# Gated attention and MLP: a redesign in head quads with row strips, column strips and VectorE chords, where GpSimd makes the two shifted copies of each VectorE pair

## Chip, cores and metric

The kernel runs on one core of one Trainium2 chip. The metric is device time in microseconds (us) of one execution. Engines in the profile: PE is TensorE's matmuls, PEld its weight loads, DVE is VectorE, ACT is ScalarE, POOL is GpSimd, SP is the engine that issues most DMAs.

## What is computed

```python
B, S, D = 1, 2048, 640          # F = 1536, H = 32 heads, Dh = 20; all bf16
def _A_ref(x, wqkv, wo):
    qkv = (x @ wqkv).reshape(B, S, 3, H, Dh).transpose(2, 0, 3, 1, 4)
    q, k, v = qkv[0], qkv[1], qkv[2]
    scores = jnp.einsum("bhqd,bhkd->bhqk", q, k) * Dh ** -0.5
    p = softmax(scores, axis=-1)
    o = jnp.einsum("bhqk,bhkd->bhqd", p, v)
    return o.transpose(0, 2, 1, 3).reshape(B, S, D) @ wo
def _B_ref(x, w1, b1, w2):
    h = x @ w1 + b1
    return (h * jnp.tanh(softplus(h))) @ w2          # mish
x = A_x
g = sigmoid((x * gate_w).sum(-1, keepdims=True))
return g * _A_ref(x, A_wqkv, A_wo) + (1 - g) * _B_ref(x, B_w1, B_b1, B_w2)
```

The bulk is the attention: 32 heads x 2048 x 2048 scores, each of which needs an exponential. In tiles of 128 keys x 1024 (two heads x 512 queries, a "pair" below) these are 1024 pairs.

## The kernel before, in words

x is brought in transposed by one DMA (`xT`, feature on partitions). The queries are cut into four chunks of 512 (`qc`), the heads into 16 groups of two (`emit_group`). For a group the loop over `NS` = 16 key blocks makes one pair per step, in this order on PE: two score matmuls into PSUM (L395; the heads' 20 features lie on 20 of the 128 partitions, at partitions `base` and `base + 32`, so the two are row strips of the array), then eight accumulating matmuls (L412) with the pair's exponentials as weights (128x128 each) and 21 columns of V moving (20 features and a column of ones that gives the softmax denominator). Between them ACT takes the exponential of all 1024 columns in one instruction (L406). `aps` holds two score tiles and `e_pool` two exponential tiles. At a group's end DVE takes reciprocals of the denominators and scales (L421, L423).

All other work is cut into units that stand in a list: projections of Q, K and V (`qt_unit` L208, `kt_units` L143, `v_units` L186), the MLP's first matmul with its mish (`mlp_ht_unit` L223: an Exp on ACT, L231, and five DVE instructions, among them a reciprocal at L241), its second matmul (`mlp_b_units` L261), and the transposes and output projection of the query chunk before (L288, L304, L318). `pump_slot` is called after each pair with a credit of 340 or 460 and emits units by a cost written with each. So PE's order is the program's order: a pair, then some units, then a pair. Projections of K and V for a head quad are done once, in the first query chunk. The softmax scale is applied inside the exponential. Weights come by DMA from ACT's, SP's and GpSimd's queues.

Of the kernel before, what the change touches and what calls it, by code (L numbers as in the profile page):

```python
# [8 lines left out]
P = 128  # L10
ACT = mybir.ActivationFunctionType
ALU = mybir.AluOpType
F32 = mybir.dt.float32
BF16 = mybir.dt.bfloat16


@with_exitstack
def kernel(
# [12 lines left out]
    nc = tc.nc  # L31

    _, S, D = A_x.shape
    F = B_w1.shape[1]
    H = 32
    DH = D // H
    KT = D // P
    FT = F // P
    NS = S // P
    QC = 512  # L40
    NQC = S // QC
    NU = QC // P
    NPAIR = H // 4
    NG = H // 2
    ROWB = 32
    inv_sqrt_dh = float(DH) ** -0.5
    CB = 512
    CH = CB // 2

    x2d = A_x[0]  # L50
    out2d = out[0]

    consts = ctx.enter_context(tc.tile_pool(name="consts", bufs=1))
    wqp = consts.tile([P, KT, NPAIR, P], BF16, tag="wqp")
    ident = consts.tile([P, P], BF16, tag="ident")
    wo_sb = consts.tile([P, KT, D], BF16, tag="wo_sb")
    w1_sb = consts.tile([P, KT, F], BF16, tag="w1_sb")
    w2_sb = consts.tile([P, FT, D], BF16, tag="w2_sb")
    b1bf = consts.tile([P, FT], BF16, tag="b1bf")
    b1f = consts.tile([P, FT], F32, tag="b1f")  # L60
    g_t = consts.tile([P, NS], F32, tag="g_t")
    kT_all = consts.tile([P, NPAIR, S], BF16, tag="kT_all")
    VA = consts.tile([P, NS, H, DH + 1], BF16, tag="VA")

    aps = ctx.enter_context(tc.tile_pool(name="aps", bufs=2, space=bass.MemoryType.PSUM))
    xtc_pool = ctx.enter_context(tc.tile_pool(name="xtc", bufs=2))
    qtc_pool = ctx.enter_context(tc.tile_pool(name="qtc", bufs=3))
    e_pool = ctx.enter_context(tc.tile_pool(name="e_pool", bufs=2))
    opool = ctx.enter_context(tc.tile_pool(name="opool", bufs=1))
    otpool = ctx.enter_context(tc.tile_pool(name="otpool", bufs=1))  # L70
    actpool = ctx.enter_context(tc.tile_pool(name="actpool", bufs=1))
    mishp = ctx.enter_context(tc.tile_pool(name="mishp", bufs=2))
    bpool = ctx.enter_context(tc.tile_pool(name="bpool", bufs=2))
    smallp = ctx.enter_context(tc.tile_pool(name="smallp", bufs=2))
    dpool = ctx.enter_context(tc.tile_pool(name="dpool", bufs=1))
    outp = ctx.enter_context(tc.tile_pool(name="outp", bufs=2))

    xt_ctx = ExitStack()
    xt_ctx.__enter__()
    xtpool = xt_ctx.enter_context(tc.tile_pool(name="xtpool", bufs=1))  # L80
    xT = xtpool.tile([P, KT, S], BF16, tag="xT")

    stage_ctx = ExitStack()
    stage_ctx.__enter__()
    stpool = stage_ctx.enter_context(tc.tile_pool(name="stpool", bufs=1))
    Wq = stpool.tile([P, KT, D], BF16, tag="Wq")
    nc.scalar.dma_start(Wq, A_wqkv[:, 0:D].rearrange("(kt p) c -> p kt c", p=P))
    nc.sync.dma_start_transpose(
        out=xT[:, :, :], in_=x2d.rearrange("s (kt p) -> s kt p", p=P)
    )  # L90
    wv0 = xtpool.tile([P, KT, 4 * DH], BF16, tag="wvp", bufs=2)
    nc.scalar.dma_start(
        out=wv0[:, :, :],
        in_=A_wqkv[:, 2 * D : 2 * D + 4 * DH].rearrange("(kt p) c -> p kt c", p=P),
    )
    gw = xtpool.tile([P, KT, 1], BF16, tag="gw")
    nc.scalar.dma_start(gw, gate_w.rearrange("(kt p o) -> p kt o", p=P, o=1))
    wk0 = xtpool.tile([P, KT, P], BF16, tag="wkp", bufs=2)
    nc.gpsimd.memset(wk0, 0.0)
    for r in range(4):  # L100
        col0 = 64 * (r // 2) + ROWB * (r % 2)
        nc.scalar.dma_start(
            out=wk0[:, :, col0 : col0 + DH],
            in_=A_wqkv[:, D + r * DH : D + (r + 1) * DH].rearrange(
                "(kt p) c -> p kt c", p=P
            ),
        )
    nc.sync.dma_start(b1bf, B_b1.rearrange("(ft p) -> p ft", p=P))
    nc.gpsimd.dma_start(wo_sb, A_wo.rearrange("(kt p) c -> p kt c", p=P))
    nc.gpsimd.dma_start(w1_sb, B_w1.rearrange("(kt p) c -> p kt c", p=P))  # L110
    nc.gpsimd.dma_start(w2_sb, B_w2.rearrange("(ft p) c -> p ft c", p=P))

    nc.gpsimd.memset(wqp, 0.0)
    for h in range(H):
        p, r = divmod(h, 4)
        col0 = 64 * (r // 2) + ROWB * (r % 2)
        nc.gpsimd.tensor_copy(
            out=wqp[:, :, p, col0 : col0 + DH],
            in_=Wq[:, :, h * DH : (h + 1) * DH],
        )  # L120
    stage_ctx.__exit__(None, None, None)
    make_identity(nc, ident)
    nc.vector.tensor_copy(b1f, b1bf)
    nc.gpsimd.memset(VA, 1.0)

    def kt_units(p, wk=None):
        if wk is None:
            wk = xtpool.tile([P, KT, P], BF16, tag="wkp", bufs=2)
            nc.gpsimd.memset(wk, 0.0)
            for r in range(4):  # L130
                h = 4 * p + r
                col0 = 64 * (r // 2) + ROWB * (r % 2)
                nc.sync.dma_start(
                    out=wk[:, :, col0 : col0 + DH],
                    in_=A_wqkv[:, D + h * DH : D + (h + 1) * DH].rearrange(
                        "(kt p) c -> p kt c", p=P
                    ),
                )

        def chunk(sc):  # L140
            pk = aps.tile([P, CB], F32, tag="t")
            for kt in range(KT):
                nc.tensor.matmul(  # L143
                    pk[:, 0:QC],
                    lhsT=wk[:, kt, 0:P],
                    rhs=xT[:, kt, sc * QC : (sc + 1) * QC],
                    start=(kt == 0),
                    stop=(kt == KT - 1),
                )
            nc.vector.tensor_copy(  # L150
                out=kT_all[:, p, sc * QC : (sc + 1) * QC], in_=pk[:, 0:QC]
            )

        return [(1200, (lambda sc=sc: chunk(sc))) for sc in range(NQC)]

    def v_units(p, wv=None):
        if wv is None:
            wv = xtpool.tile([P, KT, 4 * DH], BF16, tag="wvp", bufs=2)
            nc.sync.dma_start(
                out=wv[:, :, :],  # L160
                in_=A_wqkv[:, 2 * D + 4 * p * DH : 2 * D + 4 * (p + 1) * DH].rearrange(
                    "(kt p) c -> p kt c", p=P
                ),
            )

        def unit(st):
            pv = aps.tile([P, CB], F32, tag="t")
            for kt in range(KT):
                lhsT = xT[:, kt, st * P : (st + 1) * P]
                if p == 0:  # L170
                    nc.tensor.matmul(  # L171
                        pv[:, 0 : 4 * DH],
                        lhsT=lhsT,
                        rhs=wv[:, kt, :],
                        start=(kt == 0),
                        stop=False,
                    )
                    nc.tensor.matmul(
                        pv[:, 4 * DH : 4 * DH + 1],
                        lhsT=lhsT,  # L180
                        rhs=gw[:, kt, 0:1],
                        start=False,
                        stop=(kt == KT - 1),
                    )
                else:
                    nc.tensor.matmul(  # L186
                        pv[:, 0 : 4 * DH],
                        lhsT=lhsT,
                        rhs=wv[:, kt, :],
                        start=(kt == 0),  # L190
                        stop=(kt == KT - 1),
                    )
            nc.vector.tensor_copy(  # L193
                out=VA[:, st, 4 * p : 4 * p + 4, 0:DH],
                in_=pv[:, 0 : 4 * DH].rearrange("p (h d) -> p h d", d=DH),
            )
            if p == 0:
                nc.scalar.activation(
                    g_t[:, st : st + 1], pv[:, 4 * DH : 4 * DH + 1], ACT.Sigmoid
                )  # L200

        return [(260, (lambda st=st: unit(st))) for st in range(NS)]

    def qt_unit(p, xTc, qTc_p):
        def unit():
            pq = aps.tile([P, CB], F32, tag="t")
            for kt in range(KT):
                nc.tensor.matmul(  # L208
                    pq[:, 0:QC],
                    lhsT=wqp[:, kt, p, 0:P],  # L210
                    rhs=xTc[:, kt, 0:QC],
                    start=(kt == 0),
                    stop=(kt == KT - 1),
                )
# [312 lines left out]
```

## Time and profile before

| | |
|---|---|
| runs | 1384.87, 1419.17, 1405.74 us; median 1405.74 |
| the profiled execution | span 1383.0 us from its first to its last instruction; its time around the span is not listed, and the nearest run, 1384.87, is 1.9 over it |
| exponentials (L406, ACT) | 1024 x 1022 ns |
| score matmuls (L395, PE) | 2048 in 1024 strips of two, 589.2 us busy |
| accumulating matmuls (L412, PE) | 8192 x 182 ns, 398.1 us busy |
| reciprocal of the MLP (L241, DVE) | 96 x 1744 ns |
| DMA | 16.91 MB, at 185 GB/s in the first fortieth of the span, 1 to 21 GB/s after the second |

The page gives for every engine its busy time and its share of the span, and cuts the span into 40 slices in which each digit is a tenth. PEclk is the clock granted to TensorE, in tenths of full. Groups of instructions give line, engine, operation, output and inputs with shapes, count, busy time and mean duration, and behind the bar the idle time before them with what ended it. Matmuls overlap in the array, so durations of single matmuls add up to more than the time they take; start-to-start distances are read from the timeline.

### The profile page before, as it was taken

How to read it: one execution, taken by the hardware profiler on the slowest of the kernel's cores; microseconds unless marked ns; L12 is line 12 of the kernel's file. 1: busy time of each engine (PE TensorE's matmuls, PEld its weight loads, DVE VectorE, ACT ScalarE, POOL GpSimd, SP SyncE). 2: the span in 40 equal slices, each digit the busy share in tenths (PEclk: the TensorE clock that was granted, in tenths of full speed). 3: DMA queues.
4: the chain of work that ended last, by engine and by line, in shares of the span. 5: the costliest groups of instructions: out<-in, count | busy, mean ns of one | idle time of the engine just before them, and what ended most of it. 6: DMA issues, size and time to landing. Idle time of an engine off the chain costs nothing.

```text
span 1383.0 us, 28359 instructions
## 1 busy us (share of the span) xinstructions
PE 1235.3 (89%) x12384; PEld 589.6 (43%) x12384; DVE 463.9 (34%) x1093; ACT 1053.3 (76%) x1138; POOL 28.6 (2%) x51
## 2 busy tenths in 40 slices
PE   0699999988999988998889998998889988998887
PEld 0354444544444444443434444443434444453333
DVE  0222222377722576410101477410001476510002
ACT  0286666987768877698998777698998787699995
POOL 7000000000000000000000000000000000000000
PEclk9975555975585555795555555695555555695555
DMA  9600000000000000000000000000000000000000
GB/s 185 109 8 7 8 7 7 2 1 1 13 8 11 11 1 1 1 21 1 1 1 11 11 1 1 1 2 1 1 2 6 16 2 1 1 2 1 1 1 20
DMA packets 53086, 16.91 MB, mean 12 GB/s; under 512 B 49408, under 2 KB 52096, under 8 KB 52960
## 3 DMA queue, kind: packets, MB, share of 16 engines
q1 hardware_dynamic: 47456, 9.30, 4.6%
q0 software_dynamic: 912, 4.75, 1.2%
q10 hardware_dynamic: 4592, 1.03, 0.6%
q8 instruction: 97, 1.59, 0.5%
q14 instruction: 29, 0.24, 0.1%
HBM read 7.21 MB, written 2.62 MB: 7 GB/s over the span
## 4 chain that ended last, share of the span: by engine, by line
PE 67%; ACT 25%; issue 3%; DMA 3%; DVE 1%; ACTq 0%
PE Sp L395 26%; ACT E L406 25%; PE acc L412 15%; PE ph L223 8%; PE pk L143 5%; PE pb L261 4%; DMA xT<-in_A_x_dram 3%; PE pq L208 3%; PE pa L304 3%; PE pv L186 3%; PE pt L288 1%; ACTq L406 0%; PE pv L171 0%; ACT e_sb L231 0%; DVE d L311 0%
## 5 line engine op out<-in xcount | busy, mean ns | idle before, releaser
L406 ACT ACTIVATE E<-Sp 128x1024 bf16<-128x1024 f32 x1024 | 1006.0, 1022 | 223.6 <-PE Sp L395 213.0
L395 PE MATMUL Sp<-qTc_p,kT_all 20*128 20x512 bf16 x2048 | 589.2, 559 | 0.0
L412 PEld LDWEIGHTS <-E 128*128 128x128 bf16 x8192 | 335.7, 106 | 471.1 <-ACT E L406 376.9
L412 PE MATMUL acc<-VA,E 128*128 128x21 bf16 x8192 | 398.1, 182 | 95.5 <-ACT E L406 93.5
L241 DVE RECIPROCAL rd<-rd 128x256 f32<-128x256 f32 x96 | 167.4, 1744 | 0.8
L395 PEld LDWEIGHTS <-kT_all 20*128 20x128 bf16 x2048 | 104.3, 98 | 51.5 <-issue 18.2
L223 PE MATMUL ph<-xTc,w_sb 128*128 128x256 bf16 x480 | 119.0, 403 | 0.1
L421 DVE RECIPROCAL rden<-acc 128x8 f32<-128x8 f32 x64 | 12.4, 193 | 297.4 <-PE acc L412 297.4
L223 PEld LDWEIGHTS <-w_sb 128*128 128x128 bf16 x480 | 51.7, 128 | 57.4 <-issue 42.6
L234 DVE SCALAR_TENSOR_TENSOR e_sb<-e_sb 128x256 f32<-128x256 f32 x96 | 40.4, 421 | 100.5 <-ACT e_sb L231 99.6
L215 DVE CAST qTc_p<-pq 128x512 bf16<-128x512 f32 x32 | 22.1, 691 | 148.8 <-PE Sp L395 98.6
L231 ACT ACTIVATE e_sb<-ph,b1f 128x256 f32<-128x256 f32 x96 | 45.4, 473 | 33.8 <-PE ph L223 29.9
L143 PE MATMUL pk<-xT,wk 128*128 128x512 bf16 x140 | 66.0, 548 | 0.0
L208 PE MATMUL pq<-xTc,wqp 128*128 128x512 bf16 x160 | 64.5, 492 | 0.0
L261 PE MATMUL pb<-w_sb,actT 128*128 128x512 bf16 x192 | 58.0, 419 | 0.1
L150 DVE CAST kT_all<-pk 128x512 bf16<-128x512 f32 x32 | 22.1, 691 | 96.3 <-PE pk L143 96.3
L186 PE MATMUL pv<-wv,xT 128*128 128x80 bf16 x560 | 50.7, 237 | 0.0
L193 DVE CAST VA<-pv 128x80 bf16<-128x80 f32 x128 | 30.4, 243 | 57.7 <-PE pv L186 51.5
L143 PE MATMUL pk<-xT,wk_118 128*128 128x512 bf16 x20 | 7.2, 544 | 44.4 <-DMA xT<-in_A_x_dram 44.4
L243 DVE SCALAR_TENSOR_TENSOR actT<-ph,b1f,rd 128x256 bf16<-128x256 f32 x96 | 45.8, 478 | 0.1
L186 PEld LDWEIGHTS <-xT 128*128 128x128 bf16 x560 | 33.4, 117 | 23.2 <-issue 23.0
L261 PEld LDWEIGHTS <-actT 128*128 128x128 bf16 x384 | 28.5, 101 | 33.3 <-issue 24.1
(101 smaller groups left out, 351.9 us busy)
## 6 DMA issues: line engine op xcount, KB each, us to landing
w_sb<-in_B_w_dram POOLq DMA_DIRECT2D x2, 1920.0 KB, 31.1
out_dram<-ot SPq DMA_DIRECT2D x16, 160.0 KB, 1.8
Wq<-in_A_wqkv_dram ACTq DMA_DIRECT2D x1, 800.0 KB, 4.9
wo_sb<-in_A_wo_dram POOLq DMA_DIRECT2D x1, 800.0 KB, 24.5
wv<-in_A_wqkv_dram SPq DMA_DIRECT2D x7, 100.0 KB, 2.3
wk<-in_A_wqkv_dram SPq DMA_DIRECT2D x28, 25.0 KB, 2.6
wv_114<-in_A_wqkv_dram ACTq DMA_DIRECT2D x1, 100.0 KB, 10.7
wk_118<-in_A_wqkv_dram ACTq DMA_DIRECT2D x4, 25.0 KB, 29.7
```

The lines of the kernel that those rows point to most:

```text
L143: nc.tensor.matmul(pk[:, 0:QC], lhsT=wk[:, kt, 0:P], rhs=xT[:, kt, sc * QC : (sc + 1) * QC], start=(kt == 0), stop=(kt == KT - 1),)
L186: nc.tensor.matmul(pv[:, 0 : 4 * DH], lhsT=lhsT, rhs=wv[:, kt, :], start=(kt == 0), stop=(kt == KT - 1),)
L208: nc.tensor.matmul(pq[:, 0:QC], lhsT=wqp[:, kt, p, 0:P], rhs=xTc[:, kt, 0:QC], start=(kt == 0), stop=(kt == KT - 1),)
L223: nc.tensor.matmul(ph[:, 0:CH], lhsT=w1_sb[:, kt, ft * P : (ft + 1) * P], rhs=xTc[:, kt, half * CH : (half + 1) * CH], start=(kt == 0), st ...
L231: nc.scalar.activation(e_sb, ph[:, 0:CH], ACT.Exp, bias=b1f[:, ft : ft + 1], scale=1.0)
L241: nc.vector.reciprocal(out=rd, in_=rd)
L243: nc.vector.scalar_tensor_tensor(out=actT[:, ft, half * CH : (half + 1) * CH], in0=ph[:, 0:CH], scalar=b1f[:, ft : ft + 1], in1=rd, op0=AL ...
L261: nc.tensor.matmul(tile_[:, 0 : col1 - col0], lhsT=actT[:, ft, u * P : (u + 1) * P], rhs=w2_sb[:, ft, col0:col1], start=(ft == 0), stop=(f ...
L304: nc.tensor.matmul(pa[:, :], lhsT=oT[:, ct, u * P : (u + 1) * P], rhs=wo_sb[:, ct, 0:CB], start=(ct == 0), stop=(ct == KT - 1),)
L395: nc.tensor.matmul(Sp[:, QC * t : QC * (t + 1)], lhsT=kT_all[base + ROWB * t : base + ROWB * t + DH, p, j * P : (j + 1) * P,], rhs=qTc_p[b ...
L406: nc.scalar.activation(E[:, :], Sp[:, :], ACT.Exp, scale=inv_sqrt_dh)
L412: nc.tensor.matmul(acc[:, u, t, 0 : DH + 1], lhsT=E[:, QC * t + P * u : QC * t + P * (u + 1)], rhs=VA[:, j, h, 0 : DH + 1], start=first, s ...
```

## The change

The kernel body is written anew. What it does:

- **Opening.** x comes in its own layout in seven plain DMAs and is transposed by PE (80 transposes) into `xT`. The weights come whole, from SP's queue.
- **Head quads.** Four heads lie on the four 32-partition strips of `kT` and `qT` (20 features, then zeros). A pass (`try_pass`, `score_mms`, L609) issues two score matmuls for one pair, or four for two pairs (heads 0 and 1 of the quad, "L", and heads 2 and 3, "R"). Key and query strips are made 128 rows at a time, written to DRAM and read back strip by strip.
- **Two kinds of exponential.** A pair in `SA` or `SB` goes to ACT (L985, as before). A pair in `SD` goes to DVE (L996): one tensor_scalar adds a bias to the scaled score, clamps at zero and converts to int16, whose bits read as bf16 are a chord of the exponential. GpSimd adds two constants to those integers (L1003, `Z[1]` and `Z[2]`), and the three tiles together stand for the exponential. Three sets of such tiles exist (`NZ`), eight tiles for ACT's (`NE`).
- **Column strips.** V with its column of ones is the weight (128 x 32), the exponentials move (512 columns), and the four heads of the quad accumulate in the four 32-partition strips of one PSUM bank (L738). An ACT pair is accumulated once, a DVE pair three times. All other matmuls but the transposes are also cut into four 32-column strips (`mm4`, L255).
- **Group end.** DVE copies the accumulator to SBUF, the denominators go to DRAM and back as 128x16, DVE takes the reciprocal, they go to DRAM and back spread over 32 partitions a head, and GpSimd multiplies (L786). The result goes to DRAM and is read back into `xT` for the output projection.
- **MLP.** Mish is an ACT function on 128x3072, four times for each half of the sequence; DVE adds the bias before it.
- **Order.** A planner at build time walks through time with a cost written for each operation (below), picks for each engine the next ready operation by priority or due time, and emits the whole program in that order. It also decides which pairs go to DVE, and chunk by chunk where the other work goes.

By the instruction order of the changed kernel: 733 pairs go to ACT and 291 to DVE; 731 score passes, of which 439 have two matmuls, 291 four and one six; 3212 accumulating matmuls; 582 shifted copies and 32 multiplications on GpSimd.

```diff
+LAT = 0.12
...
+SHIFTS = (35.0, 83.0)
+ZBIAS = 128.0 * 127 - 251.8
+ADDS_ON_POOL = True
...
+    NE, NZ = 8, 3
...
+    def mm4(outs_, lhs, rhs, start, stop):
+        for k in range(4):
+            nc.tensor.matmul(
+                outs_[k], lhsT=lhs[k], rhs=rhs[k], start=start, stop=stop,
+                tile_position=(0, 32 * k),
+            )
+    C4 = 0.225
...
+        return [
+            lambda t=t, k=k: nc.tensor.matmul(
+                S_[:, k * QC : (k + 1) * QC],
+                lhsT=kT[32 * t : 32 * t + 32, j * P : (j + 1) * P],
+                rhs=qT[32 * t : 32 * t + 32, g.c * QC : (g.c + 1) * QC],
+                start=True, stop=True, tile_position=(32 * t, 0),
+            )
+            for k, t in enumerate((t0, t0 + 1))
+        ]
...
+        op = Op("ACT", 0.946, None, [score], prio=3)
...
+        op = Op("DVE", 1.19, None, [score], prio=3)
...
+    def pe_start(now, dur, m, fn):
+        if mode[0] != m:
+            dur += 0.1
...
+                    lambda t=t, k=k, e=e, st=st, sp=end_ty: nc.tensor.matmul(
+                        acc[32 * t : 32 * t + 32, :],
+                        lhsT=VAs[(g.q // 2) % 2][:, e["j"], g.q % 2, t, :],
+                        rhs=e["ap"][:, k * QC : (k + 1) * QC],
+                        start=st, stop=sp, tile_position=(0, 32 * t),
+                    )
...
+            mu = new("POOL", 1.25, lambda: nc.gpsimd.tensor_tensor(out=o, in0=a, in1=rb, op=ALU.mult), d4, prio=0)
...
+                op.fn = lambda: nc.vector.tensor_scalar(
+                    out=Z[0], in0=SD, scalar1=ZBIAS, scalar2=0.0, op0=ALU.add, op1=ALU.max)
...
+                for k in range(2):
+                    if ADDS_ON_POOL:
+                        a = Op("POOL", 1.05, lambda k=k: nc.gpsimd.tensor_scalar(
+                            out=Z[k + 1], in0=Z[0], scalar1=SHIFTS[k], scalar2=1.0, op0=ALU.add, op1=ALU.mult), [op], prio=1)
+                    else:
+                        a = Op("DVE", 0.34, lambda k=k: nc.vector.tensor_scalar(
+                            out=Z[k + 1], in0=Z[0], scalar1=SHIFTS[k], scalar2=None, op0=ALU.add), [op], prio=2)
```

## The prediction

> **What bounds the kernel now.** I read the page's first two parts, then the costliest groups, then the timeline at two clocks, then the opening and GpSimd's few rows.
>
> ```profile
> span 1383.0 us, 28359 instructions
> ...
> PE 1235.3 (89%) x12384; PEld 589.6 (43%) x12384; DVE 463.9 (34%) x1093; ACT 1053.3 (76%) x1138; POOL 28.6 (2%) x51
> ...
> PEclk9975555975585555795555555695555555695555
> ```
>
> PE is busy 89% of the span, mostly at half clock, and ACT 76%: neither is full, since a pair goes PE, ACT, PE through two buffers and the projections and MLP stand between the pairs in PE's order. The timeline at half clock shows the alternation (start, length, what; in brackets what ended the idle time):
>
> ```profile
> 705.59 0.39 PE L412 MATMUL acc<-VA,E 128*128 128x21 bf16 x8 [0.25 <-ACT E L406]
> 705.91 0.61 PE L395 MATMUL Sp<-qTc_p,kT_all 20*128 20x512 bf16 x2
> ...
> 706.62 1.95 ACT L406 ACTIVATE E<-Sp 128x1024 bf16<-128x1024 f32 x2 [0.16 <-PE Sp L395]
> ```
>
> PE waits for ACT, then ACT for PE. Two exponentials back to back take 1.95, one 1.02 (L406's mean), so their distance is 0.93. The next timelines give PE's distances at full and at half clock:
>
> ```profile
> 601.82 0.39 PE L395 MATMUL Sp<-qTc_p,kT_all 20*128 20x512 bf16 x2
> 602.14 0.82 PE L208 MATMUL pq<-xTc,wqp 128*128 128x512 bf16 x3
> 602.80 0.35 PE L412 MATMUL acc<-VA,E 128*128 128x21 bf16 x8
> ```
> ```profile
> 748.16 0.61 PE L304 MATMUL pa<-wo_sb,oT_prev 128*128 128x512 bf16 x1
> 748.57 0.31 PE L318 MATMUL pa_9692<-wo_sb,oT_prev 128*128 128x128 bf16 x1
> ```
>
> Three 512-column matmuls start within 0.66, 0.22 each, at full clock; 0.41 at half. The two score strips run at the same time, but the next full-height matmul starts 0.32 after them: 0.10 is lost in changing over. Before a score pair about 0.08 is lost (705.59 to 705.91 is 0.32, eight starts at 0.03 are 0.24).
>
> ```profile
> 120.00:240.00 120.00, 120.00 (x1083) 54.85 (x1082) 27.41 (x94) 75.26 (x75) 1.89 (x3) 0.50 0.07 7
> 580.00:620.00 40.00, 38.98 (x489) 20.26 (x485) 5.68 (x18) 38.85 (x41) 0.00 (x0) 0.96 0.08 18
> ```
>
> These are stretches with busy time of PE, PEld, DVE, ACT, POOL, then the clock: 0.50 in the first although PE never rests, 0.96 in the second. In the first, 85 projections of 512 columns, 255 of 80, 149 score strips (20 of 128 rows, so 80 columns' worth each) and 594 x 21 columns fill 88,300 of 144,000 half-clock column times, 61%. In the second, 81 matmuls of at most 512, 82 score strips and 326 x 21 fill at most 57% of full. GpSimd's rows, with the opening:
>
> ```profile
> 4.21 4.38 POOL L113 MEMSET wqp<- 128x5120 bf16 x1
> ...
> 8.66 6.85 POOL L117 COPY wqp<-Wq 128x100 bf16<-128x100 bf16 x32
> 15.55 0.28 POOL masks.py:199 TENSOR_SCALAR_AFFINE_SELECT ident<-ident 128x128 bf16<-128x128 bf16 x1
> 15.79 9.05 POOL L124 MEMSET VA<- 128x10752 bf16 x1
> ```
> ```profile
> 0.75 43.62 DMA xT<-in_A_x_dram
> ```
>
> **The change part by part.** *ACT.* 733 exponentials x 0.93 = 682. Mish: from L406 (1024 elements, 1022 ns) and L231 (256, 473) an element costs 0.715 ns, so 3072 take 2.49, x 8 = 20. Five table loads at 1.28 (the length of the load before) are 6, twelve evictions in the opening at 0.6 are 7. Sum 715, against 1053.
>
> *PE, full clock.* Passes: 731 x (0.22 + 0.18 changeover) = 292, taking four strips to run at once as two do. Accumulations: 3212 matmuls go out in 880 calls of two to four strips, x 0.22 = 194. No column strips stand in this trace; they cost 0.22 a call if they run at once like row strips (taken, as both are strips of one array) and 0.22 a matmul if not. Projections, MLP, output: 2992 strips of 512 in fours, 748 x 0.22 = 165. 1280 strips of 160 (V): starts of 0.03, 320 x 0.12 = 36. 1152 strips of 128: 288 x 0.11 = 32. Transposes 80 x 0.1 = 8. Sum 727; with column strips one after the other 6204 x 0.22 = 1365 stands in place of 359 and the sum is 1733. At half clock (0.41): 431 + 361 + 307 + 43 + 35 + 8 = 1185.
>
> *DVE.* From 128x512 in 691 ns (L150) and 128x128 in 291 (L269) an element costs 1.04 ns, so 1024 take 1.23; 291 x 1.23 = 358. Some 150 evictions of 512 at 0.69 are 104, the smaller ones about 40. Sum 500, under the others; the MLP's 167 of reciprocal goes. It is hidden under PE, and if that cover went it would still be 200 short.
>
> *GpSimd.* 582 copies of 128x1024 int16 and 32 products. The trace has no arithmetic of this size. Memsets give 4.66 for 5632 elements, 0.83 ns each. Copies of 100 start every 0.215, the select of 128 takes 0.24 to the next start. If all beyond memset speed is fixed, a shifted copy costs 0.83 x 1.024 + 0.13 = 0.98. If all but a start of 0.03 goes by the element (1.8 ns), it costs 1.88. A line through the copy and the select (0.9 ns) gives 1.05, the value I take, since both read and write as the new operation does. A product reads two operands: between 0.56 and 1.9, taken 1.1. Sum 582 x 1.05 + 35 = 646, at the upper end 1094 + 60 = 1154. A copy's delay sits on a path too: PE's order holds the accumulation of `Z[2]` in place, and whatever stands behind it, the next score pass too, waits; ACT lives meanwhile from its two score tiles.
>
> The Trainium skill (GPSIMD Engine Reference, Performance versus the Vector engine, Engine selection) speaks against this use: elementwise arithmetic belongs on VectorE, GpSimd takes 2.6 cycles of 1.2 GHz an element with two inputs, though with one input about line rate. By its two-input figure, an estimate, a copy would take 2.22 and GpSimd's sum with the ends below would be about 1370; no row here shows such a price.
>
> *Ends.* The first exponential now starts at 64.35, behind the 43.6 transposing load. Plain loads of 160 KB land in 1.8 (`out`) and 100 KB in 2.3 (`wv`), so the first four tiles are there by about 5; four transposes with evictions (4) and two projections at half clock (5) put it near 16. At the end, after the last pass: eviction 0.7, four DMA hops at about 2 are 8, a product 1.1, five output units alternating 1.3 PE and 0.7 DVE are 10, the last store 1.8: 22, of which 4 to 6 are PE work already counted; net 18. DMA otherwise has room: 1 to 21 GB/s are used.
>
> *Sum.* Three engines come out near each other: PE 727, ACT 715, GpSimd 646, each in a fixed order with at most three to eight tiles between them. So none will run full; before, the fullest ran at 89%. 727 / 0.89 = 817, with 16 + 18 the span is 851, and with the 2 that the nearest run lies over its span 853: I say **850**. The profile before stands 1.6% under its median (1383.0 to 1405.74).
>
> **The rivals.** *A (0.57): as summed.* At 97% fill it is 784, at 80% 943.
>
> *B (0.19): GpSimd is the bound.* A copy between 1.35 and 1.88: 582 x 1.35 + 35 + 36 = 857, at 1.6 about 1010, at 1.88 1190. For it: the copy row allows it, and A leaves GpSimd only 0.3 a copy of room. Against: select and copy differ by 28 elements and only 0.025.
>
> *C (0.13): the clock stays low.* 1185 / 0.97 + 34 = 1256 at half clock throughout, (851 + 1256) / 2 = 1053 if half the time. For it: PE was busy without pause at 0.50 in the first stretch. Against: at half clock the new work fills (880 + 748) x 0.41 and 292 whole and 439 half passes, 878 of 1185 with V and the rest left out, 74%, more than the 61% that did not lift it; at full clock the same work at 0.22 is 471 of 851, 55%, in the neighbourhood of what held 0.96. The Trainium skill (TensorE: Matmul & The Clock Gate, Part 1) lets sustained PE activity open the clock. By it the sum stays at 853; the first stretch speaks against busyness alone.
>
> *D (0.09): slower, by one mechanism.* A shifted copy costs so much that GpSimd's queue alone is longer than the kernel before: 582 x p + 45 + 36 passes 1406 at p = 2.28 and 1434 at 2.33; at 2.5 it gives 1536. For it: int16 in and out with two operations was never timed here, and every Z2 holds up PE's order. Against: it needs 2.2 ns an element, beyond the 1.8 that the copies bound.
>
> *E (0.02): column strips run singly*, PE 1733 + 34, about 1770; the row strips that do run at once speak against it.
>
> **How the numbers follow.** Best single time 850. Below 770 lies about 0.04 (A nearly full), above 1220 a third of C with D and E, 0.16; so 770 to 1220. A measurement of this kernel tells 2% from no change (its runs spread by 2.4%). Faster by over 2%: A, B and C, 0.89; within 2%: 0.02 of D; slower: the rest of D and E, 0.09.
>
> **What would show it.** In the changed profile: L1003 near 1.05 mean and POOL near 75% busy (B: over 90%, and PE's accumulation waiting for POOL; D: POOL about 100% with copies over 2.3). PEclk 9 in most slices (C: 5). L985 idle a tenth of its time, ended by the score passes. The first exponential near 16. Row passes 0.40 to the next matmul, four accumulating strips starting within 0.22. I am wrong if the span is over 950 at full clock with copies near 1.05: then the fixed order itself loses more than the 11% taken.

## The result, and the profile after

The changed kernel takes 857.64 us (median of 4 runs, 856.22 to 860.18) against 1411.78 before; the ratio is 0.6211, 95% interval 0.6169 to 0.6252. The profiled execution took 857.08 with a span of 855.3.

The page's first two parts, where the lines shown of before had PE at 89%, ACT at 76% and mostly half clock:

```profile
span 855.3 us, 25648 instructions
...
PE 782.1 (91%) x10764; PEld 274.3 (32%) x10764; DVE 497.4 (58%) x586; ACT 731.3 (86%) x758; POOL 665.9 (78%) x632
...
POOL 6267999857995999976798799987729999989930
PEclk9999999999999999999999999999969999999999
```

Four engines are now above half busy, TensorE's clock is full but in one slice (620 to 641, 0.67), and GpSimd has long stretches at 9 with dips between. The groups of the two kinds of exponential and of the copies:

```profile
L1003 POOL TENSOR_SCALAR Z<-Z 128x1024 int16<-128x1024 int16 x582 | 609.1, 1047 | 140.7 <-DVE Z L996 91.8
L996 DVE TENSOR_SCALAR Z<-SD 128x1024 int16<-128x1024 f32 x291 | 355.4, 1221 | 187.0 <-PE SD L609 80.5
L985 ACT ACTIVATE E<-SA 128x1024 bf16<-128x1024 f32 x367 | 379.5, 1034 | 36.9 <-PE acc L738 18.7
...
L786 POOL TENSOR_TENSOR OT<-accS,rdB 128x512 bf16<-128x512 f32 x32 | 40.9, 1279 | 27.2 <-DMA rdB<-rD 25.4
```

A copy is 1047 ns long (1.05 was taken), a chord 1221 (1.23), a product 1279 (1.1). The timeline of TensorE, to be read against the one at full clock before:

```profile
400.91 0.39 PE L609 MATMUL SD<-qT,kT 32*128 32x512 bf16 x1
...
401.24 0.61 PE L738 MATMUL acc<-E,VA 128*32 128x512 bf16 x6
...
401.82 0.39 PE L609 MATMUL SB<-qT,kT 32*128 32x512 bf16 x2
402.14 0.83 PE L255 MATMUL misc<-w,hid 128*32 128x512 bf16 x12
402.91 0.39 PE L609 MATMUL SA<-qT,kT 32*128 32x512 bf16 x2
```

A pass of four strips (400.91) and one of two (401.82) both let the next matmul start 0.32 to 0.33 later. Twelve column strips, three calls of four, take 0.77 to the next pass, 0.22 each with 0.10 for the changeover: four strips do run at once. GpSimd's timeline over 30 us:

```profile
300.00 21.31 POOL L1003 TENSOR_SCALAR Z<-Z 128x1024 int16<-128x1024 int16 x19
321.27 1.27 POOL L786 TENSOR_TENSOR OT<-accS,rdB 128x512 bf16<-128x512 f32 x1
322.63 7.80 POOL L1003 TENSOR_SCALAR Z<-Z 128x1024 int16<-128x1024 int16 x7
```

This is the line that the prediction lacked: nineteen copies take 21.31 although each lasts 1.05, so their distance is (21.31 - 1.05) / 18 = 1.126, 7% over the duration. GpSimd's queue is 582 x 1.126 + 32 x 1.35 = 698 us long, and here it has no gap: in the whole trace 509 of the 581 distances between copies are this one. The Trainium skill (Perfetto Trace Analysis, GPSIMD Engine Instruction) says that GpSimd's reported spans are not to be relied on and that start-to-start distances are; the rows above agree, 1.126 against 1.047.

Two lines of the waits (who waited for whom, total us, times, longest) are needed below:

```profile
DVE Z L996 <- POOL Z L1003: 78.6, 71, 2.4
PE acc L738 <- POOL Z L1003: 16.5, 47, 2.0
```

The span divides into three: the first exponential starts at 18.9, the last ends at 816.6, and 38.7 follow.

### The profile page after: what moved, and what is told of

It reads as the page before. It is cut to its first block, busy times and chain, and to the rows that moved or that the text cites. A ratio compares the mean times of both kernels' runs of the same rounds, so it can differ in the third digit from the quotient of the medians.

```text
span 855.3 us, 25648 instructions
## 1 busy us (share of the span) xinstructions
PE 782.1 (91%) x10764; PEld 274.3 (32%) x10764; DVE 497.4 (58%) x586; ACT 731.3 (86%) x758; POOL 665.9 (78%) x632
## 5 line engine op out<-in xcount | busy, mean ns | idle before, releaser
L1003 POOL TENSOR_SCALAR Z<-Z 128x1024 int16<-128x1024 int16 x582 | 609.1, 1047 | 140.7 <-DVE Z L996 91.8
L996 DVE TENSOR_SCALAR Z<-SD 128x1024 int16<-128x1024 f32 x291 | 355.4, 1221 | 187.0 <-PE SD L609 80.5
L985 ACT ACTIVATE E<-SA 128x1024 bf16<-128x1024 f32 x367 | 379.5, 1034 | 36.9 <-PE acc L738 18.7
L985 ACT ACTIVATE E<-SB 128x1024 bf16<-128x1024 f32 x366 | 378.6, 1034 | 33.8 <-PE acc L738 16.9
L738 PE MATMUL acc<-Z,VA 128*32 128x512 bf16 x1746 | 259.7, 384 | 22.0 <-POOL Z L1003 16.5
L738 PE MATMUL acc<-E,VA 128*32 128x512 bf16 x1466 | 219.2, 386 | 1.6 <-DVE accS L765 0.9
L609 PEld LDWEIGHTS <-kT 32*128 32x128 bf16 x2048 | 82.8, 91 | 255.5 <-issue 239.5
L738 PEld LDWEIGHTS <-VA 128*32 128x32 bf16 x3212 | 94.2, 94 | 179.3 <-issue 161.6
L609 PE MATMUL SB<-qT,kT 32*128 32x512 bf16 x732 | 145.4, 384 | 3.4 <-ACT E L985 1.3
L609 PE MATMUL SA<-qT,kT 32*128 32x512 bf16 x734 | 145.0, 384 | 3.5 <-ACT E L985 1.5
L609 PE MATMUL SD<-qT,kT 32*128 32x512 bf16 x582 | 114.4, 385 | 0.1
L255 PE MATMUL misc<-w,hid 128*32 128x512 bf16 (+1 forms) x1536 | 92.8, 305 | 3.7 <-DVE nat L401 2.9
L255 PE MATMUL misc<-xT,w 128*32 128x512 bf16 x960 | 85.8, 383 | 1.0 <-DVE VA L332 0.6
L255 PE MATMUL misc<-xT,wqk 128*32 128x512 bf16 x820 | 66.3, 392 | 13.8 <-DVE nat L401 8.8
L786 POOL TENSOR_TENSOR OT<-accS,rdB 128x512 bf16<-128x512 f32 x32 | 40.9, 1279 | 27.2 <-DMA rdB<-rD 25.4
L255 PEld LDWEIGHTS <-xT 128*32 128x32 bf16 x1920 | 38.1, 95 | 40.3 <-issue 33.3
L453 DVE TENSOR_SCALAR hid<-misc,b 128x512 bf16<-128x512 f32 x48 | 35.8, 746 | 21.7 <-PE misc L255 21.2
L255 PE MATMUL misc<-wo_n,xT 128*32 128x512 bf16 (+1 forms) x640 | 30.4, 300 | 11.8 <-DVE hid L854 11.8
L255 PEld LDWEIGHTS <-hid 128*32 128x32 bf16 x1536 | 32.1, 96 | 25.4 <-issue 21.1
L255 PE MATMUL misc<-wv,xT 128*32 128x160 bf16 (+1 forms) x1280 | 38.4, 235 | 1.0 <-ACT qT L297 0.7
L255 PEld LDWEIGHTS <-wqk 128*32 128x32 bf16 x880 | 22.0, 97 | 41.6 <-issue 34.9
L854 DVE SCALAR_TENSOR_TENSOR hid<-misc,gate,hid 128x128 bf16<-128x128 f32 (+1 forms) x32 | 16.5, 547 | 24.5 <-PE misc L255 24.3
```

The lines of the kernel that those rows point to most:

```text
L255: nc.tensor.matmul(outs_[k], lhsT=lhs[k], rhs=rhs[k], start=start, stop=stop, tile_position=(0, 32 * k),)
L453: return lambda: nc.vector.tensor_scalar(out=o, in0=bk, scalar1=b1[:, ft : ft + 1], scalar2=None, op0=ALU.add)
L609: lambda t=t, k=k: nc.tensor.matmul(S_[:, k * QC : (k + 1) * QC], lhsT=kT[32 * t : 32 * t + 32, j * P : (j + 1) * P], rhs=qT[32 * t : 32 * ...
L738: lambda t=t, k=k, e=e, st=st, sp=end_ty: nc.tensor.matmul(acc[32 * t : 32 * t + 32, :], lhsT=VAs[(g.q // 2) % 2][:, e["j"], g.q % 2, t, : ...
L786: mu = new("POOL", 1.25, lambda: nc.gpsimd.tensor_tensor(out=o, in0=a, in1=rb, op=ALU.mult), d4, prio=0)
L854: nc.vector.scalar_tensor_tensor(out=bgl[:, s, c0:c1], in0=src, scalar=gate[:, 0, s : s + 1], in1=bgl[:, s, c0:c1], op0=ALU.mult, op1=ALU.add)
```

## The experiments

My theory T was the prediction's: TensorE's fixed order sets the steady part and GpSimd runs beside it. Rival R: GpSimd sets the pace. All experiments start from the changed kernel. The runs went in three sets, each on one chip: e1 to e4; e5 to e7 with the changed kernel once more; e9 to e12. The kernel before took 1338, 1347 and 1371 at its best beside them, while the changed kernel took 857.64 and 859.27: so its relatives are compared by their times, and a ratio holds within its set. The sets with e1 to e4 and e9 to e12 do not hold the changed kernel itself; in the latter e11 has its order and takes 857.05.

**e1: the copies left out, same order.**

```diff
-a = Op("POOL", 1.05, lambda k=k: nc.gpsimd.tensor_scalar(out=Z[k + 1], ...), [op], prio=1)
+a = Op("POOL", 1.05, None, [op], prio=1)
...
-... "ap": Z[k + 1].bitcast(BF16), "tok": t})
+... "ap": Z[0].bitcast(BF16), "tok": t})
```

> The 582 shifted copies are left out and the accumulation reads the unshifted tile three times, so the softmax is another one; the order on all other engines is the same. Theory T (TensorE's fixed order sets the steady part, GpSimd at 78% busy runs beside it): TensorE waited for copies for 16.5 us in all and VectorE's chord for GpSimd 79, of which little is on the path: 835 to 857. Rival R (GpSimd sets the pace, as its 92% busy stretches suggest): with 666 us of work gone the time falls to what TensorE alone needs, 782 busy at 97% in the middle, 800 or less.

Measured: 815.05 (814.33 to 816.43), 42.6 less. That is between the two, and beyond what T allowed. The first exponential starts at 17.2 in place of 18.9 and the last ends at 775.0 in place of 816.6, so 39.8 of it lie in the steady part. Stretches of both kernels (busy time of PE, PEld, DVE, ACT, POOL, then the clock), first after, then e1:

```profile
60.00:600.00 540.00, 518.63 (x6938) 174.39 (x6930) 331.81 (x377) 494.30 (x514) 448.65 (x424) 1.00 0.13 35
```
```profile
60.00:600.00 540.00, 516.19 (x7104) 170.12 (x7107) 346.28 (x395) 508.15 (x531) 29.34 (x23) 0.99 0.13 36
```

PE's busy time hardly differs, yet it gets through 7104 matmuls in place of 6938, 2.4% more, and ACT through 531 instructions in place of 514. A busy PE in this view holds pipeline tails and small waits, since the ends of matmuls are modelled.

The starts show where the time lies. Both traces hold the same 10764 matmuls, all but 12 records in the same order, so the distance of each from the one before it can be subtracted, matmul by matmul. The differences sum to 42.3 us. Some 240 accumulating matmuls that read a shifted copy, and start less than 0.1 us after that copy is done, hold 52.9 us; all other distances together are 10.6 shorter than in e1. So what the copies cost is the time that TensorE, in its fixed order, stands before a copy that is not there yet. The wait line above shows 16.5 of these 52.9, the rest is hidden in "busy". That GpSimd's copies slow VectorE's own work is ruled out as a cause: the chord takes 1221 ns with the copies and 1220 without.

**e2: the second copy made twice.**

```diff
-lambda k=k: nc.gpsimd.tensor_scalar(out=Z[k + 1], ...)
+lambda k=k: [nc.gpsimd.tensor_scalar(out=Z[k + 1], ...) for _ in range(k + 1)]
```

> The second shifted copy of each pair is made twice over, 873 copies in place of 582, in the same order. GpSimd's work becomes 873 x 1.047 + 41 = 955 and with the ends of 19 and 20 that do not hold copies about 995 to 1010, if the sum of rival B in the prediction is right that GpSimd's queue bounds as soon as a pair costs over 2.7 us. If copies were hidden by a wider margin than the sum says (TensorE or ScalarE wait for each other anyway): under 930. If each copy's delay adds in full to the path, as R says: 857 + 291 x 1.05 = 1160.

Measured: 1133.89 (two executions), near R's 1160 and well over the 995 to 1010 that the sum of rival B gave. 291 copies more cost 276, 0.95 each, where 1.12 would be the whole of each. Two lines of e2's waits (who waited for whom, total us, times, longest):

```profile
PE acc L738 <- POOL Z L1003: 200.3, 237, 3.4
DVE Z L996 <- POOL Z L1003: 197.8, 104, 5.1
```

In the changed kernel the first stood at 16.5; the second is not what it seems (e11). Subtracted matmul by matmul from the changed kernel's trace, e2 is 278 us longer, and 220 of them lie before accumulations that a copy released; the rest is spread over all matmuls, at a clock of 0.90 in place of 0.99. The sum fell short for three reasons that its trace shows: distance and not duration (873 x 0.08 = 70), longer ends (18 and 48, where 39 in all had been taken), and the rest, some 35, in which this queue itself stood.

**e3: the copies on VectorE** (the branch that was there).

```diff
-ADDS_ON_POOL = True
+ADDS_ON_POOL = False
```

> The two shifted copies are made by VectorE instead (the branch that is there already); the planner then gives 282 pairs to VectorE and 742 to ScalarE. GpSimd is left with 32 products. Theory T: no great change, 835 to 880, as long as a copy on VectorE costs no more than the 0.34 written in the plan (VectorE then at 497 + 564 x 0.34 = 689). If it costs as much per element as the chord does (1.2 us, no faster for 16-bit data in SBUF), VectorE's sum is 497 + 677 = 1170 and the time about 1220. Rival R: with GpSimd's pace gone the time falls under 820.

Measured: 833.01, 25 less than the changed kernel. T's lower edge is 835, R's upper 820: neither. A copy on VectorE costs 442 ns, a little over the plan's 0.34:

```profile
L1006 DVE TENSOR_SCALAR Z<-Z 128x1024 int16<-128x1024 int16 x564 | 229.5, 442 | 8.9
```

VectorE rises to 691.6 of 829.3 busy, which gives back part of e1's 43. So the part of the change that puts the copies on GpSimd costs 25 us against the same redesign with them on VectorE, planned anew with 9 pairs fewer there. The Trainium skill (GPSIMD Engine Reference, Engine selection) prefers VectorE for elementwise work; here the measured prices are 1047 and 442 ns and the kernel goes with the page.

**e4: three banks for the output projection at the end.**

```diff
-toks = Mpool.toks if opening[0] else Mpool.toks[:1]
+ended = min(ptr.values()) >= NQ * NQC * NS and (SDtok.free(now) or SDtok.idx == "end")
+if ended:
+    SDtok.idx = "end"
+toks = Mpool.toks if opening[0] or ended else Mpool.toks[:1]
```

> Once all score passes are out, the output projection may use the two banks of the chord's score tile as well as its own one; before, its units go through one bank and take 2.33 us each (TensorE 1.5, then VectorE 0.75) for some 35 us behind the last exponential. Theory (the tail of 39 is this single bank): a unit then takes 1.5, the last 14 units gain about 0.8 each but the last five still wait for the denominators, so 8 to 14 us less: 843 to 850. Rival (the tail is the denominators' way through DRAM, 13 us, and the output stores): no change, 855 to 860.

Measured: 848.48 (846.2 to 849.87), 9 to 11 less, as the theory said. VectorE's evictions in the tail, first after, then e4:

```profile
844.79 0.75 DVE L854 SCALAR_TENSOR_TENSOR hid<-misc,gate,hid 128x512 bf16<-128x512 f32 x1 [1.58 <-PE misc L255]
847.12 0.75 DVE L854 SCALAR_TENSOR_TENSOR hid<-misc,gate,hid 128x512 bf16<-128x512 f32 x1 [1.58 <-PE misc L255]
```
```profile
840.62 0.75 DVE L854 SCALAR_TENSOR_TENSOR hid<-SD,gate,hid 128x512 bf16<-128x512 f32 x1 [1.35 <-PE SD L255]
841.92 0.75 DVE L854 SCALAR_TENSOR_TENSOR hid<-misc,gate,hid 128x512 bf16<-128x512 f32 x1 [0.54 <-PE misc L255]
```

The distance of two units falls from 2.33, matmuls and eviction one after the other through one bank, to 1.30, the matmuls alone. The last chunk still waits for its denominators.

**e5: four sets of chord tiles, planned anew.**

```diff
-NE, NZ = 8, 3
+NE, NZ = 8, 4
```

> Four sets of chord tiles in place of three (room for them from three output tiles that nothing uses). The copies start 1.11 us apart, so GpSimd's queue holds 582 x 1.11 + 41 = 687 of 855. Theory L (the 42 us that the copies cost come from VectorE and TensorE waiting for one particular copy, with sets that come free late): a fourth set lets a chord start before the oldest copy is used, and 10 to 25 us go: 833 to 848. Theory Q (the queue itself is the bound in the stretches that are 92% busy): the copies are as long as before and the time stays at 850 to 862.

Measured: 869.63, ten more, outside both expectations. The planner used the fourth set to give 311 pairs to VectorE in place of 291: 40 copies more for GpSimd, 40 x 1.126 = 45 us. The run mixes the two; by e11 the fourth set alone changes nothing, so the ten go with the new plan.

**a0: the changed kernel again**, beside e5 to e7.

> The changed kernel itself, once more, beside the next ones on the same chip: 850 to 865 by every theory.

Measured: 859.27 (857.64 to 860.83), ratio 0.6377 (0.6352 to 0.6403), the before of this set being quicker.

**e6: all pairs on ScalarE.**

```diff
-dt = SDtok if SDtok.free(now) else None
+dt = None
```

> No pair goes to VectorE: ScalarE takes all 1024, there are no chords and no copies, each pair is accumulated once, and the planner makes 778 score passes. ScalarE: 1024 x 0.92 + 35 = 977, TensorE 778 x 0.40 + 512 x 0.22 + 240 = 665. If ScalarE then bounds nearly full (97%) with the ends of 19 and 39: about 1065. If the fixed order keeps every engine near 90% as before: about 1140. If the chords had bought nothing (TensorE's extra accumulations eat their gain): near 860.

Measured: 1062.34 (two executions), ratio to before 0.7884 (0.785 to 0.7918), as the sum for a ScalarE at 97% said (ACT is busy 991.1 of 1059.7). Beside a0's 0.6377, the strips, the layout and the planner alone bring 0.212 of the 0.362 that the change takes off, and the chords the other 0.151, or 1062.34 - 859.27 = 203 us. The clock of e6 is another one:

```profile
PEclk9999999999999999997999655555555555557775
```

Over 600 to 640 it is 0.50 although TensorE counts as busy for 35.8 of the 40 us, with 170 matmuls (the changed kernel gets through 6938 in 540 us). So the strips alone do not keep the clock up. ScalarE is busy 97% from 640 to 1020 all the same, so it bounds e6 at either clock.

**e7: copies on VectorE, three banks, and one eviction for the last projections.** The first two are e3 and e4; the third:

```diff
-while k0 < 4:
-    ...
-    nc.vector.tensor_scalar(out=n[32 * k0 : 32 * k1, :], in0=b[32 * k0 : 32 * k1, :], scalar1=scal[k0], ...)
+nc.vector.tensor_scalar(out=n, in0=b, scalar1=scl[:, 0:1], scalar2=None, op0=ALU.mult)
```

> Three edits together: the copies on VectorE, three banks for the output projection after the last pass, and the last projections' evictions (four instructions of 32 rows at 0.71 us, for which TensorE waited 2.9 us each of four times) as one instruction with a scale per partition. Their gains apart are 24, 9 and an estimated 8 (four waits of 2.9 less four of 0.75); if they lie in different stretches and add: 857 - 41 = 816, range 808 to 826. If the copies' stalls and the last projections' overlap: 825 to 835.

Measured: 813.61 (812.64 to 817.21), ratio 0.6047 (0.6009 to 0.6086): the fastest kernel of the study, faster than before and after. The gains of e3 (25 to 26) and e4 (9 to 11) make 34 to 37 of the 46 to a0; the third edit, which was not run alone, and the new plan share the rest. The third edit answers one place in the changed kernel's trace, at 612 to 631, where TensorE sat idle four times behind small evictions and the clock then fell, to 0.67 over 620 to 641. TensorE's timeline there, with the idle time before the matmul in brackets:

```profile
620.12 1.26 PE L255 MATMUL misc<-xT,wqk 128*32 128x512 bf16 x20 [2.94 <-DVE nat L401]
```

**e9: two numbers of the plan.**

```diff
-a = Op("POOL", 1.05, ...        mu = new("POOL", 1.25, ...
+a = Op("POOL", 1.12, ...        mu = new("POOL", 1.3, ...
```

> Only two numbers of the plan are changed: a copy is planned at 1.12 (the measured distance of copies) in place of 1.05, a product at 1.3 in place of 1.25; the planner then gives 284 pairs to VectorE and 740 to ScalarE, and puts the waits where GpSimd really is. Theory Q (GpSimd runs some 6% behind the plan and TensorE, in a fixed order, waits for it): with 14 copies less and the order fitted, 5 to 20 us go: 838 to 852. Theory N (the plan's number does not matter, since the queue of copies is simply long): 855 to 862.

Measured: 839.77 (837.72 to 841.36), 18 to 20 less with no other edit. 14 copies less are 14 x 1.126 = 16 us of GpSimd's queue. Whether the fitted order adds to that was not parted.

**e10: one copy on each engine**, with e7's other two edits.

```diff
-if ADDS_ON_POOL:
+if k == 1:
```

> VectorE makes the first shifted copy of each pair, GpSimd the second (planned at 0.42 and 1.12), with three banks and the single eviction of e7; 291 pairs on VectorE. GpSimd: 291 x 1.12 + 41 = 367; VectorE: 498 + 291 x 0.41 = 617. If the copies' price is GpSimd's queue alone, it is gone here as in e7, and VectorE is freer: 805 to 815. If any copy that comes back from GpSimd costs TensorE a wait: 820 to 835.

Measured: 824.96, in the second range: with half the copies, GpSimd is idle half the time, and still the kernel is 11 over e7 (in another set). The copies of both engines became longer:

```profile
L1009 POOL TENSOR_SCALAR Z<-Z 128x1024 int16<-128x1024 int16 x291 | 354.3, 1217 | 356.3 <-DVE Z L1002 344.5
L1012 DVE TENSOR_SCALAR Z<-Z 128x1024 int16<-128x1024 int16 x291 | 150.6, 518 | 9.0
```

GpSimd's take 1217 ns in place of 1047, VectorE's 518 in place of the 440 of e7. The two hold each other up. GpSimd's copies are 1.28 long in the median, and the 7 of 291 that no copy of VectorE overlaps are 1.05; 58 of VectorE's last from 0.6 to 1.55, and every one of these starts while GpSimd is at a copy or a product. How much of the 11 this is was not parted.

**e11: e5's fourth set, the order kept.**

```diff
-Z = Zs[t.idx]
+Z = Zs[znext[0] % (NZ + 1)]
+znext[0] += 1
```

> The order of the changed kernel is kept to the instruction, with 291 pairs on VectorE, and only the tiles rotate through four sets in place of three. It parts the two changes that lay together in e5 (a set more, and 20 pairs more on VectorE, 40 copies more on GpSimd). Theory Q (the queue's length): 850 to 860. Theory L (VectorE's chord waits 76 us for GpSimd's last copy out of the set that it writes over): those waits go and 10 to 25 us with them, 835 to 849.

Measured: 857.05, no change, as theory Q said. Theory L falls. The chord's wait for GpSimd (78 us in all) stays as well, and the changed kernel's trace says why: it is no wait for a copy. One of these waits and the score pass of the same chord:

```profile
303.90 1.23 DVE L996 TENSOR_SCALAR Z<-SD 128x1024 int16<-128x1024 f32 x1 [1.62 <-POOL Z L1003]
```
```profile
303.37 0.38 PE L609 MATMUL SD<-qT,kT 32*128 32x512 bf16 x1
```

The chord starts 0.53 after its own score pass. Over all the waits put down to GpSimd the median of this distance is 0.52 us, and it is 0.52 where the wait is put down to the score pass. So VectorE waits for TensorE, which stands before its accumulations (e1), and a set more does not help it.

**e12: e7 with measured costs in the plan.**

```diff
-Op("ACT", 0.946, ...   Op("DVE", 1.19, ...   Op("DVE", 0.34, ...
+Op("ACT", 0.92, ...    Op("DVE", 1.22, ...   Op("DVE", 0.42, ...
```

> e7 with three numbers of the plan set to what was measured: ScalarE's exponential 0.92 (planned 0.946), the chord 1.22 (1.19), VectorE's copy 0.42 (0.34). The planner moves a few pairs. If the fixed order's loss comes from plans that do not fit: 800 to 811. If it does not: 811 to 818.

Measured: 828.16 to 834.25 in three executions, ratio 0.6016 (0.5949 to 0.6083) in its set: some 15 us over e7's time, against both expectations. The planner gave only 259 pairs to VectorE. A plan with truer numbers is not by itself a faster one; why this one loses was not followed up. The fourth execution took 1244.59, and the trace kept is of that one: in its tail six calls of four strips take 2.78 us, where they take 1.30 in e4, although its clock record reads 1.00 throughout. Its cause is open, and nothing else is read from it.

## Why the prediction held, step by step

- *The time*: 850 was said, 857.64 measured, in case A. Two terms missed in opposite ways: the steady part was 798 (18.9 to 816.6) where 817 was taken, the ends 18.9 and 38.7 where 16 and 18 were. That they cancel to within 5 us of the span is luck. The steady part was summed with the 89% at which the kernel before ran, a share taken over from another order: 727 / 798 is 91%, but without the copies (e1) it is 96%, and ScalarE alone (e6) runs at 97%. A fixed order does not as such cost 11%.
- *TensorE's sum* (727 of work; passes 0.22 + 0.18; column strips at once; full clock): the prices are shown by the timeline at 400.91 to 402.91, the clock by PEclk; in the sum, 320 x 0.12 is 38 and not 36. Rivals C and E did not come. That the new work would keep the clock up is borne out at 0.992 over the execution; the one dip follows idle time (612 to 631). The argument for it, how much of the array the work fills, agrees with e6, where fewer matmuls of the same kind stood at 0.50, but no run varied this alone.
- *ScalarE*: 715 was summed, 731.3 is busy. Back to back, exponentials stand 0.91 apart (0.93 taken), but one that stands alone is busy for its whole 1.02.
- *VectorE*: 500 and 497.4.
- *GpSimd*: the price of one copy, 1.05, was right as a duration; as a distance it is 1.126, so the queue is 698 and not 646. This is the mis-sized term. It matters, since the prediction laid the loss of 11% to a fixed order in general. It did name the path, an accumulation that waits for `Z[2]` and holds up all behind it, but gave it no number. e1 gives it: 42.6 in all, 52.9 before accumulations that a copy released. e2 shows that 291 copies more cost almost their full length; e9, with 14 fewer and another order, takes 18 less. So GpSimd, meant to lie beside TensorE, holds it back at 78% busy, and rival B's mechanism was partly at work inside case A's number.
- *The end*: the prediction charged one chunk's five units at 2 us. In the trace the units of three chunks follow one another after the last exponential, mostly 2.33 apart through one bank; e4 gets 9 to 11 of it back.
- *The opening* came three late, but not by the loads (whose 1.8 was the row of a store, `out`). The first four tiles were in transposition by 6.13. The plan then put four more transposes ahead of the first projection, and the first of these waited for its tile until 8.37; three more stood between the two projections, at 11.53 and 15.69. The prediction counted four transposes in all.

```profile
8.37 0.72 PE L269 MATMUL misc<-ident,hid 128*128 128x128 bf16 x5 [1.50 <-DMA hid<-in_A_x_dram]
...
11.53 2.32 PE L255 MATMUL SD<-xT,wqk 128*32 128x512 bf16 x20 [0.84 <-ACT xT L274]
```

- *ScalarE idle a tenth of its time*: 8% of the span in front of L985, but ended by accumulations for 35.6 us (35 times) and by score passes for 26.3 (57 times): a tile of exponentials comes free only when its accumulation, which may stand behind a copy, is done. Right in size, half right in cause.

## What to carry to other kernels

When several engines come out close to each other in a sum, do not take the one with the shortest sum as hidden if others wait for its results: price its queue by start-to-start distance. A busy share of 78% does not tell of room if the idle time lies in a few stretches and the rest is full. To see who holds whom, leave the work out and keep the order to the instruction (e1), rather than let a planner redistribute it (e5); then subtract the two traces start by start. A wait list can name the wrong engine (e11) and can miss waits that lie inside busy time (e1).

## What the runs showed of the hardware

- A tensor_scalar of 128x1024 int16 in SBUF takes 1047 ns on GpSimd, 1.126 from one to the next, and 442 ns on VectorE, where the same number of elements from PSUM takes 1221.
- Where copies of GpSimd and VectorE overlap (e10), GpSimd's takes 1.28 us in the median in place of 1.05.
- A product of two 128x512 float32 operands on GpSimd takes 1279 ns, 2.4 times a copy per element.
- Four 32-column strips of 512 take 0.22 us together at full clock, four 32-row strips as long as two.
- Memsets on GpSimd of 128 columns strided by 32 took 654 ns where 128 contiguous ones took 205.
